# All query chunks weighed with v stationary, and their sums turned back into rows by 64-row transposes

## The chip, the cores and the metric

The kernel runs on one core of a Trainium2 chip. The metric is the device time of one execution in microseconds (us). The time before is 2366.17 us, the median of 3 runs (2365.53 to 2366.57).

## The reference

An attention without softmax, whose output goes through a mixture of experts that takes the best expert alone. Cut to what matters here:

```python
B, S, D, d_qk = 8, 2496, 256, 64
scores = (1 / S) * np.matmul(z, z.transpose(0, 2, 1))    # B x S x S
attn = np.maximum(scores, 0.0) ** 2
x = (u * np.matmul(attn, v)).reshape(B * S, D)
logits = x @ w_gate + modality_bias[modality_id]         # 8 experts
e_idx = np.argmax(logits, axis=1)
# out[i] = softmax(logits[i])[e_idx[i]] * (relu(x[i] @ w1[e]) @ w2[e]), e = e_idx[i]
```

All of it is float32. The kernel gets that precision from the faster float32r products by splitting both factors into a high and a low part and adding three products (high·high, high·low, low·high).

## The kernel before, in words

**Two phases.** Phase 1 computes the attention, the logits and the routing, and scatters the rows by expert to DRAM. Phase 2 takes tiles of 512 rows of one expert through the two layers. The change is in phase 1, but for one call in phase 2.

**Chunks and steps.** A batch entry has 2496 queries, in 5 chunks (c = 0 to 4) of 512, the last of 448. A chunk runs through its keys in 10 steps (i = 0 to 9) of two 128-key blocks, so phase 1 has 8 x 5 x 10 = 400 steps, numbered g. For a step:
- `scores` (L287) makes the products of keys and queries in 6 matmuls, 2 blocks x 3 terms, each on 64 rows of the array. The two blocks use the two halves of the array's rows (`halves`, partitions 0 to 63 and 64 to 127), so two matmuls run side by side, one in each half. ACT then applies the relu (L298) and the square (L304).
- `high` (L307) rounds the square to float32r on ACT or DVE (a table `by` chooses), and `low` (L314) takes the difference on DVE: `ah` and `al`, each 128 keys x 2 x 512 queries.
- `weigh` (L328) multiplies by v (`vh`, `vl`). The keys of the upper and lower 64 partitions are summed apart, in PSUM tiles `acc[r]` (r = 0, 1, the two halves of the array).

**Two forms of weigh.** For c < 4 (L341 to L358) the stationary operand is 128 queries of `ah` or `al` and the 256 columns of v move. The sums come out as rows (query on the partition). A step is 4 blocks of queries x 2 key blocks x 6 matmuls = 48 matmuls with 256 columns moving; the last step, whose second key block is only half real, has 36. For c = 4 (L359 to L369) the stationary operand is 128 columns of v and the 448 queries move: 24 matmuls, and the sums come out transposed (column of v on the partition).

**After a chunk.** `evacuate_low` (ACT, L391, two copies) and `evacuate_high` (DVE, L397, two additions) join the two halves' sums in the SBUF tile `x`. For c < 4, `gate_rows` (DVE, L403) then multiplies by u. For c = 4, `make_rows` (L407) turns the sums back into rows with eight 128x128 transposes on PE (L415), and `take_rows` (DVE, L422) multiplies them by u out of PSUM. Then come 16 pieces of `logits` (DVE, L432) and, once per batch entry, the routing.

**Order.** PE, ACT, DVE and POOL run in an order that the loop at L891 writes out. In iteration g it emits what is due, then `high(g+2)`, `scores(g+3)`, `low(g+2)`, `square(g+3)`, `weigh(g)` and the tasks fixed for g. The rest lies in queues with a first step and a last step, which `beside` empties as its estimates of ACT's and DVE's load allow. PSUM has one `s` tile of two banks and six banks for `acc`, of which a chunk takes four; the transposes take two of the same six.

Of the kernel before, what the change touches and what calls it, by code (L numbers as in the profile page):

```python
# [15 lines left out]
P = 128  # L16
T = 512
# [9 lines left out]
def tile_attention_moe(ctx: ExitStack, tc: tile.TileContext, u, v, zt, mid, wg, mb, w1, w2, out):  # L27
# [300 lines left out]
    def weigh(g):  # L328
# [6 lines left out]
        def terms(k):  # L335

            if k == NCOL - 1:
                return ((0, ah, 0), (1, ah, 0), (0, ah, 1))
            return tuple((r, x, y) for x, y in ((ah, 0), (ah, 1), (al, 0)) for r in range(2))

        if c < NCH - 1:  # L341

            for m in range(J):
                o = [acc[b, c][r][m // 2][:, m % 2 * D:(m % 2 + 1) * D] for r in range(2)]
                q = slice(m * P, (m + 1) * P)
                for t in range(2):
                    k = 2 * i + t
                    begins, ends = k == 0 and m % 2 == 0, k == NCOL - 1 and m % 2 == 1
                    for n, (r, x, y) in enumerate(terms(k)):
                        nc.tensor.matmul(  # L350
                            out=o[r],
                            lhsT=x[halves[r], t, q],
                            rhs=V[b, k // J][y][halves[r], k % J, :],
                            start=begins and n < 2,
                            stop=ends and y == 1 - r,
                            skip_group_check=True,
                        )
            return  # L358
        for dh in range(KD):  # L359
            for t in range(2):  # L360
                k = 2 * i + t
# [9 lines left out]

    oT, X, LG = {}, {}, {}

    EV = {}

    def evacuate_low(b, c, h):

        w = width[c]
        if not h:
            x = rows.tile([P, J, XW], F32, tag="x", bufs=NCH + 1, name="x")  # L380
            if c < NCH - 1:
                EV[b, c] = [x[:, 2 * n:2 * n + 2, 0:D] for n in range(J // 2)]
                X[b, c] = x
            else:
                t = x.rearrange("p j c -> p (j c)")[:, 0:KD * T].rearrange("p (k t) -> p k t", k=KD)
                nc.gpsimd.memset(t[:, :, w:T], 0.0)
                EV[b, c] = [t[:, n, :w] for n in range(KD)]
                oT[b, c] = (t, x)
        o = acc[b, c][1][h]
        o = o.rearrange("p (j d) -> p j d", d=D) if c < NCH - 1 else o[:, :w]  # L390
        nc.scalar.copy(out=EV[b, c][h], in_=o)  # L391

    def evacuate_high(b, c, h):
        o = acc[b, c][0][h]
        o = o.rearrange("p (j d) -> p j d", d=D) if c < NCH - 1 else o[:, :width[c]]
        y = EV[b, c][h]
        nc.vector.tensor_tensor(out=y, in0=o, in1=y, op=ALU.add)  # L397
        if h:
            acc.pop((b, c))

    def gate_rows(b, c):
        x, ut = X[b, c], U.pop((b, c))
        nc.vector.tensor_tensor(out=x[:, :, 0:D], in0=x[:, :, 0:D], in1=ut, op=ALU.mult)  # L403

    turned_rows = {}

    def make_rows(b, c):  # L407
        t, x = oT.pop((b, c))
        parts = []
        for h in range(J // 2):  # L410
            pt = bank_tile([P, 2, D], "po")
            for jj in range(2):
                for dh in range(KD):
                    j = 2 * h + jj
                    nc.tensor.transpose(out=pt[:, jj, dh * P:(dh + 1) * P], in_=t[:, dh, j * P:(j + 1) * P], identity=ident)  # L415
            parts.append(pt)
        turned_rows[b, c] = (parts, x)

    def take_rows(b, c):
        (parts, x), ut = turned_rows.pop((b, c)), U.pop((b, c))  # L420
        for h, pt in enumerate(parts):
            nc.vector.tensor_tensor(out=x[:, 2 * h:2 * h + 2, 0:D], in0=pt, in1=ut[:, 2 * h:2 * h + 2, :], op=ALU.mult)  # L422
        X[b, c] = x

    def logits(b, c, n):

# [241 lines left out]
    def at(g, f, *args):  # L668
        tasks.setdefault(g, []).append((f, args))
# [14 lines left out]
    for b in range(B):  # L684
# [9 lines left out]
        for c in range(NCH):  # L694
            g = g0 + c * NI
            at(g + 5, load_u, b, c)
            at(g + NI - 1, evacuate_low, b, c, 0)
            at(g + NI - 1, evacuate_low, b, c, 1)
            queue(g + NI, g + NI, dve(0.7, evacuate_high, b, c, 0))
            queue(g + NI, g + NI, dve(0.7, evacuate_high, b, c, 1))  # L700
            if c == NCH - 1 and b < B - 1:
                at(g + NI + 1, make_rows, b, c)
                queue(g + NI + 2, g + NI + 3, dve(1.4, take_rows, b, c))
            elif c < NCH - 1:
                queue(g + NI, g + NI + 1, dve(1.25, gate_rows, b, c))
            if b < B - 1 or c < NCH - 1:
                for n in range(LGN):
                    last = c == NCH - 1
                    queue(g + NI + (3 if last else 1), g + NI + (3 + n // 3 if last else 5 + n // 2), dve(0.35 * LG_STEP, logits, b, c, n))

    def routing(b):

# [322 lines left out]
            scatter(B - 1, k)  # L1035

    between[0][0] = [lambda: make_rows(B - 1, NCH - 1)]
    between[0][1] = [lambda: take_rows(B - 1, NCH - 1)]
# [60 lines left out]
```

## Time and profile before

| | us |
|---|---|
| median of the runs | 2366.17 |
| the profiled execution's own time | 2354.86 |
| its span, first to last instruction | 2353.1 |
| PE busy | 2312.9 (98%) |
| ACT busy | 1586.5 (67%) |
| DVE busy | 1558.6 (66%) |
| first weigh matmul of phase 1 / last | 17 / 1400 |

The profiled execution took 11.31 us less than the median of the runs. Busy time is the time in which an engine had an instruction in flight. Matmuls overlap in flight, so how fast PE goes is read from the starts of its instructions in the timeline, not from their durations.

### The profile page before, as it was taken

The page shows a single profiled execution, that of the slowest core. Times are in us where ns is not written, and L with a number is a line of the kernel's source. Part 1 is how long each engine was busy: PE and PEld are TensorE (multiplying, and loading weights), DVE is VectorE, ACT ScalarE, POOL GpSimd, SP SyncE. Part 2 cuts the span into 40 slices and gives each one's busy share as a digit, 9 for nine tenths or more (in the row PEclk, how much of TensorE's full clock was granted, in tenths as well). Part 3 has the DMA queues.
Part 4 walks back from the last instruction along what each step waited for, and adds up shares of the span by engine and source line. Part 5 has one row for each costly group of instructions (what it writes and reads, how often), then busy time and mean ns, then how long its engine had stood idle before and what let it go on. Part 6 is the DMA issues. An engine that isn't in the chain of part 4 may idle for free.

```text
span 2353.1 us, 58980 instructions
## 1 busy us (share of the span) xinstructions
PE 2312.9 (98%) x24092; PEld 2115.4 (90%) x24092; DVE 1558.6 (66%) x4305; ACT 1586.5 (67%) x1961; POOL 355.5 (15%) x350
## 2 busy tenths in 40 slices
PE   8999999999999999999999998999999999999996
PEld 7999999999999999999999996888888888888885
DVE  6888889889889889889889776333333333333432
ACT  7999999999999999999998862333333333333332
POOL 0000210210110210210210304111111111111111
PEclk9999999999999999999999999999999999999998
DMA  5332242232332331331321123511111431111110
GB/s 180 100 107 78 84 129 68 92 115 74 105 106 70 116 109 58 114 109 60 125 82 40 57 109 137 194 54 37 55 39 53 182 123 45 46 54 37 55 33 24
DMA packets 76185, 203.13 MB, mean 86 GB/s; under 512 B 16320, under 2 KB 26048, under 8 KB 73984
## 3 DMA queue, kind: packets, MB, share of 16 engines
q1 hardware_dynamic: 60768, 157.93, 20.5%
q0 software_dynamic: 15136, 41.34, 4.7%
q8 instruction: 190, 3.11, 0.6%
q14 instruction: 91, 0.75, 0.1%
HBM read 245.96 MB, written 79.10 MB: 138 GB/s over the span
## 4 chain that ended last, share of the span: by engine, by line
PE 95%; issue 1%; ACT 1%; DMA 1%; DVE 1%; POOL 0%; SPq 0%; POOLq 0%; ACTq 0%; DVEq 0%
PE acc L350 38%; PE ph L948 18%; PE s L296 12%; PE po L961 12%; PE acc L363 7%; PE po L962 6%; PE pt L806 1%; ACT r L298 0%; PE po L415 0%; DMA xs<-x,sloti 0%; DMA out_dram<-y,ids 0%; POOL xs L530 0%; ACT ah L311 0%; DMA vr<-in_v_dram 0%; POOL out_dram L980 0%
## 5 line engine op out<-in xcount | busy, mean ns | idle before, releaser
L350 PE MATMUL acc<-vh,ah 64*128 64x256 f32 x5120 | 867.6, 281 | 0.0
L350 PE MATMUL acc<-vl,ah 64*128 64x256 f32 x4992 | 860.0, 279 | 0.0
L350 PE MATMUL acc<-vh,al 64*128 64x256 f32 x4864 | 849.7, 279 | 0.0
L350 PEld LDWEIGHTS acc<-vh,ah 64*128 64x128 f32 x5120 | 685.7, 186 | 11.2 <-DVE x L397 0.2
L350 PEld LDWEIGHTS acc<-vl,ah 64*128 64x128 f32 x4992 | 661.1, 186 | 11.5
L350 PEld LDWEIGHTS acc<-vh,al 64*128 64x128 f32 x4864 | 654.5, 187 | 0.0
L952 ACT ACTIVATE hh<-ph 128x512 fp32r<-128x512 f32 (+1 forms) x320 | 189.6, 593 | 540.5 <-PE ph L948 540.5
L953 DVE SCALAR_TENSOR_TENSOR hl<-ph,hh 128x512 fp32r<-128x512 f32 (+1 forms) x320 | 218.9, 685 | 478.4 <-ACT hh L952 478.2
L320 DVE TENSOR_TENSOR al<-r,ah 128x1024 fp32r<-128x1024 f32 (+1 forms) x360 | 431.2, 1198 | 127.7 <-ACT ah L311 122.2
L432 DVE SCALAR_TENSOR_TENSOR spare<-x,wgb 128x256 f32<-128x256 f32 x1280 | 461.3, 420 | 0.6
L948 PE MATMUL ph<-xh,w 128*128 128x512 f32 (+1 forms) x1280 | 448.5, 397 | 10.0 <-DVE hl L953 9.4
L961 PE MATMUL po<-w,hh 128*128 128x512 f32 x1264 | 454.2, 394 | 0.0
L311 ACT CAST ah<-r 128x1024 fp32r<-128x1024 f32 (+1 forms) x371 | 381.4, 1028 | 77.6 <-PE acc L350 72.6
L304 ACT ACTIVATE r<-r 128x1024 f32<-128x1024 f32 (+1 forms) x400 | 415.9, 1040 | 12.7
L296 PE MATMUL s<-zm 64*128 64x512 f32 (+1 forms) x2400 | 405.8, 392 | 11.5 <-DVE zm L256 6.0
L298 ACT ACTIVATE r<-s 128x1024 f32<-128x1024 f32 (+1 forms) x400 | 400.2, 1000 | 17.4 <-PE s L296 13.2
L530 POOL DMA_INDIRECT xs<-x,sloti x160 | 194.2, 1214 | 1072.1 <-DVE x L528 968.0
L962 PE MATMUL po<-w,hl 128*128 128x256 f32 x1264 | 354.3, 281 | 0.0
L948 PEld LDWEIGHTS ph<-xh,w 128*128 128x128 f32 x1280 | 240.6, 189 | 65.5 <-DVE hl L953 10.7
L961 PEld LDWEIGHTS po<-w,hh 128*128 128x128 f32 x1264 | 237.6, 188 | 56.3 <-issue 0.2
L296 PEld LDWEIGHTS s<-zm 64*128 64x128 f32 x2400 | 260.4, 186 | 27.9 <-ACT r L298 10.2
L980 POOL DMA_INDIRECT out_dram<-y,ids x158 | 154.1, 975 | 728.9 <-DVE y L978 695.2
(143 smaller groups left out, 2439.1 us busy)
## 6 DMA issues: line engine op xcount, KB each, us to landing
w<-w1s SPq DMA_DIRECT2D x37, 2048.0 KB
w<-w2s SPq DMA_DIRECT2D x37, 2048.0 KB
xg<-xs SPq DMA_DIRECT2D x39, 516.0 KB
vr<-in_v_dram SPq DMA_DIRECT2D x32, 512.0 KB
ut<-in_u_dram SPq DMA_DIRECT2D x32, 512.0 KB
wraw<-in_moe_w_dram SPq DMA_DIRECT2D x64, 256.0 KB
w1s<-wpair SPq DMA_DIRECT2D x32, 512.0 KB
w2s<-wpair SPq DMA_DIRECT2D x32, 512.0 KB
```

Of the source, the lines that this page charges most:

```text
L296: nc.tensor.matmul(out=s[:, t, :w], lhsT=lhs, rhs=mv[halves[t], ql, :w], start=n == 0, stop=n == 2)
L298: nc.scalar.activation(out=r[:, :, :w], in_=s[:, :, :w], func=AF.Relu, scale=INV)
L304: nc.scalar.square(out=a[:, :, :w], in_=a[:, :, :w])
L311: copy(out=ah[:, :, :w], in_=st_a[g][:, :, :w])
L320: nc.vector.tensor_tensor(out=al[:, :, :w], in0=a[:, :, :w], in1=ah[:, :, :w].bitcast(F32), op=ALU.subtract)
L350: nc.tensor.matmul(out=o[r], lhsT=x[halves[r], t, q], rhs=V[b, k // J][y][halves[r], k % J, :], start=begins and n < 2, stop=ends and y == ...
L432: nc.vector.scalar_tensor_tensor(out=spare[:, k % 2, :], in0=x[:, j, 0:D], scalar=1.0, in1=wgb[:, e, :], op0=ALU.mult, op1=ALU.mult, accum ...
L530: nc.gpsimd.indirect_dma_start(out=xs, out_offset=bass.IndirectOffsetOnAxis(ap=RT[b]["sloti"][:n, k:k + 1], axis=0), in_=x[:n, j, :], in_o ...
L948: nc.tensor.matmul(out=ph, lhsT=lhs, rhs=rhs[:, k, :], start=n == 0, stop=n == 3 * KD - 1)
L953: nc.vector.scalar_tensor_tensor(out=hl, in0=ph, scalar=0.0, in1=hh.bitcast(F32), op0=ALU.max, op1=ALU.subtract)
L961: nc.tensor.matmul(out=po[j], lhsT=hh[:, s], rhs=both, start=f == 0, stop=False, skip_group_check=True)
L962: nc.tensor.matmul(out=po[j][:, 0:D], lhsT=hl[:, s], rhs=w[:, 0, :], start=False, stop=f == KF - 1, skip_group_check=True)
```

## The change

The form of weigh with the 256 columns of v moving is removed, and all chunks take the form of c = 4, with 512 queries moving (448 for c = 4). `gate_rows` is removed. `make_rows` now serves every chunk. In place of eight 128x128 transposes it makes sixteen of 64 rows, alternating between the halves of the array, each half into a PSUM bank of its own (`parts[r]`); `take_rows` has two calls, one for each bank. `make_rows` stands one step earlier than it did for c = 4, after the first weigh of the next chunk. The logits of c < 4 may begin one step later than before, those of c = 4 one step earlier.

```diff
-        if c < NCH - 1:
-
-            for m in range(J):
-                o = [acc[b, c][r][m // 2][:, m % 2 * D:(m % 2 + 1) * D] for r in range(2)]
-                q = slice(m * P, (m + 1) * P)
-                for t in range(2):
-                    k = 2 * i + t
-                    begins, ends = k == 0 and m % 2 == 0, k == NCOL - 1 and m % 2 == 1
-                    for n, (r, x, y) in enumerate(terms(k)):
-                        nc.tensor.matmul(
-                            out=o[r],
-                            lhsT=x[halves[r], t, q],
-                            rhs=V[b, k // J][y][halves[r], k % J, :],
...
-            return
...
             x = rows.tile([P, J, XW], F32, tag="x", bufs=NCH + 1, name="x")
...
+            t = x.rearrange("p j c -> p (j c)")[:, 0:KD * T].rearrange("p (k t) -> p k t", k=KD)
+            if w < T:
                 nc.gpsimd.memset(t[:, :, w:T], 0.0)
...
+            oT[b, c] = (t, x)
+        nc.scalar.copy(out=oT[b, c][0][:, h, :w], in_=acc[b, c][1][h][:, :w])
...
+        y = oT[b, c][0][:, h, :width[c]]
+        nc.vector.tensor_tensor(out=y, in0=acc[b, c][0][h][:, :width[c]], in1=y, op=ALU.add)
...
-    def gate_rows(b, c):
-        x, ut = X[b, c], U.pop((b, c))
-        nc.vector.tensor_tensor(out=x[:, :, 0:D], in0=x[:, :, 0:D], in1=ut, op=ALU.mult)
...
     def make_rows(b, c):
         t, x = oT.pop((b, c))
-        parts = []
-        for h in range(J // 2):
-            pt = bank_tile([P, 2, D], "po")
-            for jj in range(2):
-                for dh in range(KD):
-                    j = 2 * h + jj
-                    nc.tensor.transpose(out=pt[:, jj, dh * P:(dh + 1) * P], in_=t[:, dh, j * P:(j + 1) * P], identity=ident)
-            parts.append(pt)
+        parts = [bank_tile([P, J, KD, DK], "po") for _ in halves]
+        for j in range(J):
+            for dh in range(KD):
+                for r, h in enumerate(halves):
+                    nc.tensor.transpose(out=parts[r][:, j, dh, :], in_=t[h, dh, j * P:(j + 1) * P], identity=ident[h, h])
         turned_rows[b, c] = (parts, x)
...
+    def take_rows(b, c, r):
+
+        (parts, x), ut = turned_rows[b, c], U[b, c]
+
+        def of(a):
+            return a[:, :, 0:D].rearrange("p j (k h d) -> p j k h d", k=KD, h=2)[:, :, :, r, :]
+
+        nc.vector.tensor_tensor(out=of(x), in0=parts[r], in1=of(ut), op=ALU.mult)
...
-            if c == NCH - 1 and b < B - 1:
-                at(g + NI + 1, make_rows, b, c)
-                queue(g + NI + 2, g + NI + 3, dve(1.4, take_rows, b, c))
-            elif c < NCH - 1:
-                queue(g + NI, g + NI + 1, dve(1.25, gate_rows, b, c))
             if b < B - 1 or c < NCH - 1:
+                at(g + NI, make_rows, b, c)
+                for r in range(2):
+                    queue(g + NI + 1, g + NI + 2, dve(0.7, take_rows, b, c, r))
                 for n in range(LGN):
                     last = c == NCH - 1
-                    queue(g + NI + (3 if last else 1), g + NI + (3 + n // 3 if last else 5 + n // 2), dve(0.35 * LG_STEP, logits, b, c, n))
+                    queue(g + NI + 2, g + NI + (3 + n // 3 if last else 6 + n // 2), dve(0.35 * LG_STEP, logits, b, c, n))
```

How this moves the instructions is seen at two places. The first is PE's order in the first step of chunk 1 of batch entry 0, where the rows of chunk 0 are to be made. A row gives the line, the operation, the tile written and the tiles read (the moving one first), the size of what is written, and how many follow each other. Before:

```order
L350 MATMUL acc<-vh,ah 128x256 x2
L350 MATMUL acc<-vl,ah 128x256 x2
L350 MATMUL acc<-vh,al 128x256 x2
L296 MATMUL s<-zm 128x512 x6
L350 MATMUL acc<-vh,ah 128x256 x2
L350 MATMUL acc<-vl,ah 128x256 x2
L350 MATMUL acc<-vh,al 128x256 x2
```

The same place on PE in the changed kernel, where weigh is now at L345 and the transposes at L381:

```order
L345 MATMUL acc<-ah,vh 128x512 x2
L345 MATMUL acc<-ah,vl 128x512 x2
L345 MATMUL acc<-al,vh 128x512 x2
L381 MATMUL po<-ident,x 128x64 x16
L296 MATMUL s<-zm 128x512 x6
L345 MATMUL acc<-ah,vh 128x512 x2
L345 MATMUL acc<-ah,vl 128x512 x2
L345 MATMUL acc<-al,vh 128x512 x2
```

The sixteen transposes now stand between the weigh of the new chunk's first step and the next scores, and a row of weigh writes twice as many columns as before; a step has half as many such rows.

The second place is DVE's order after the same chunk, from its two evacuations on. Before:

```order
L397 TENSOR_TENSOR x<-acc,x 128x2x256 x2
L320 TENSOR_TENSOR al<-r,ah 128x1024
L403 TENSOR_TENSOR x<-x,ut 128x4x256
L320 TENSOR_TENSOR al<-r,ah 128x1024
L432 SCALAR_TENSOR_TENSOR spare,lg<-x,wgb 128x256 x8
L320 TENSOR_TENSOR al<-r,ah 128x1024
```

In the changed kernel, where the evacuation is at L369, `take_rows` at L391 and the logits at L403, DVE has there:

```order
L369 TENSOR_TENSOR x<-acc,x 128x512 x2
L320 TENSOR_TENSOR al<-r,ah 128x1024 x2
L391 TENSOR_TENSOR x<-po,ut 128x4x2x64 x2
L320 TENSOR_TENSOR al<-r,ah 128x1024
L403 SCALAR_TENSOR_TENSOR spare,lg<-x,wgb 128x256 x8
L320 TENSOR_TENSOR al<-r,ah 128x1024
```

The one multiplication by u has become two that read PSUM, and one more `low` (L320) stands ahead of them.

More of the change, by code (lines that the diff above doesn't have):

```diff
@@ L372, in tile_attention_moe @@
     oT, X, LG = {}, {}, {}
-    EV = {}
     def evacuate_low(b, c, h):
@@ L408, in make_rows @@
         t, x = oT.pop((b, c))
[L409 to L423 removed]
+        parts = [bank_tile([P, J, KD, DK], "po") for _ in halves]
[3 more added lines that the diff above has]
+                    nc.tensor.transpose(out=parts[r][:, j, dh, :], in_=t[h, dh, j * P:(j + 1) * P], identity=ident[h, h])
+        turned_rows[b, c] = (parts, x)
+    def take_rows(b, c, r):
[3 more added lines that the diff above has]
+        nc.vector.tensor_tensor(out=of(x), in0=parts[r], in1=of(ut), op=ALU.mult)
+        if r:
+            del turned_rows[b, c], U[b, c]
+            X[b, c] = x
     def logits(b, c, n):
@@ L1037, in tile_attention_moe @@
     between[0][0] = [lambda: make_rows(B - 1, NCH - 1)]
-    between[0][1] = [lambda: take_rows(B - 1, NCH - 1)]
+    between[0][1] = [lambda: take_rows(B - 1, NCH - 1, 0), lambda: take_rows(B - 1, NCH - 1, 1)]
     for n in range(LGN):
```

18 lines of the change are left out of this document (removed).

## The prediction

> **What bounds the kernel now.** The page comes first: the span, the busy engines, the chain that ended last.
>
> ```profile
> span 2353.1 us, 58980 instructions
> PE 2312.9 (98%) x24092; PEld 2115.4 (90%) x24092; DVE 1558.6 (66%) x4305; ACT 1586.5 (67%) x1961; POOL 355.5 (15%) x350
> ...
> PE 95%; issue 1%; ACT 1%; DMA 1%; DVE 1%; POOL 0%; SPq 0%; POOLq 0%; ACTq 0%; DVEq 0%
> PE acc L350 38%; PE ph L948 18%; PE s L296 12%; PE po L961 12%; PE acc L363 7%; PE po L962 6%; PE pt L806 1%; ACT r L298 0%; PE po L415 0%; DMA xs<-x,sloti 0%; DMA out_dram<-y,ids 0%; POOL xs L530 0%; ACT ah L311 0%; DMA vr<-in_v_dram 0%; POOL out_dram L980 0%
> ```
>
> PE is 95% of the chain, and the largest line in it is the weigh that the change replaces (L350, 38%). An average over two phases hides how near the others are, so next comes the busy time of phase 1 alone (the columns are the stretch, its length, and each engine's busy time).
>
> ```profile
> 10.00:1400.00 1390.00, 1386.85 (x19319) 1334.88 (x19320) 1183.49 (x3541) 1280.19 (x1401) 179.80 (x158) 1.00 0.29 95
> ```
>
> In phase 1 ACT is busy 92% and DVE 85%. PE waits almost never, so what PE issues per step is the time, but ACT has little room.
>
> **What a step costs on PE.** The pace is in the starts of the timeline's rows (start, length, line, what, shape, count; x2 is a pair, one matmul in each half of the array). One step of chunk 0 to 3, and the scores of the steps beside it:
>
> ```profile
> 892.65 0.86 PE L296 MATMUL s<-zm 64*128 64x512 f32 x6
> 893.35 0.28 PE L350 MATMUL acc<-vh,ah 64*128 64x256 f32 x2
> 893.47 0.28 PE L350 MATMUL acc<-vl,ah 64*128 64x256 f32 x2
> ...
> 896.10 0.28 PE L350 MATMUL acc<-vh,al 64*128 64x256 f32 x2
> 896.22 0.86 PE L296 MATMUL s<-zm 64*128 64x512 f32 x6
> 896.92 0.28 PE L350 MATMUL acc<-vh,ah 64*128 64x256 f32 x2
> ...
> 903.37 0.86 PE L296 MATMUL s<-zm 64*128 64x512 f32 x6
> ```
>
> Three steps from 892.65 to 903.37 are 3.573 us each. The 24 pairs of weigh start 893.35 to 896.10, 23 gaps in 2.75: 0.1196 a pair of 256 columns. The three pairs of scores, 512 columns, take 896.22 to 896.92: 0.233 each. Chunk 4 already has the form that all chunks get, with 448 columns:
>
> ```profile
> 853.97 0.36 PE L363 MATMUL acc<-ah,vh 64*128 64x448 f32 x1
> 854.17 0.36 PE L363 MATMUL acc<-ah,vl 64*128 64x448 f32 x1
> ...
> 857.00 0.36 PE L363 MATMUL acc<-ah,vh 64*128 64x448 f32 x1
> ```
>
> From one step's first matmul to the next one's are 3.03 us for 12 pairs of weigh and 3 of scores: 0.202 a pair. So a pair costs a little more than its columns: 0.467 ns a column at 256, 0.451 at 448. That surplus is what the change saves.
>
> **Full steps of chunks 0 to 3** (32 chunks x 9 = 288). In proportion to 448, a pair of 512 columns takes 0.202 x 512/448 = 0.231. Ends: 0.2295 (64 columns more at the slope between 256 and 448, 0.43 ns) and 0.233 (the scores above). A step is then 15 x 0.231 = 3.465 (3.44 to 3.495) for 3.573: 0.108 less, x288 = **-31.1 us** (-38 to -22).
>
> The Trainium skill, "TensorE: Matmul & The Clock Gate", section "Back-to-back issue gap", speaks against this: an isolated matmul's gap is its columns at 2.4 GHz and a fixed 2.5 ns. By that halving the number of pairs saves 12 x 2.5 = 30 ns a step, 8.6 us in all. The rows disagree: 256 columns at that rate are 107 ns, and the pair took 119.6. The result by that rule stands below as a rival.
>
> **Last steps** (32). One half of the array issues 20 matmuls before and 10 after: 20 x 0.1196 - 10 x 0.231 = 0.08, **-2.6 us**.
>
> **The new transposes.** Chunk 4 shows the old ones, eight of 128x128 among 64-row work, on PE and in the weight loads (PEld):
>
> ```profile
> 887.75 0.28 PE L350 MATMUL acc<-vh,al 64*128 64x256 f32 x2
> 887.96 1.10 PE L415 MATMUL po<-ident,x 128*128 128x128 f32 x8
> 888.98 0.96 PE L296 MATMUL s<-zm 64*128 64x512 f32 x6
> 889.78 0.28 PE L350 MATMUL acc<-vh,ah 64*128 64x256 f32 x2
> ```
>
> ```profile
> 887.95 0.14 PEld L415 LDWEIGHTS po<-ident,x 128*128 128x128 f32 x1
> ```
>
> ```profile
> 887.95 0.20 PEld L415 LDWEIGHTS po<-ident,x 128*128 128x128 f32 x2
> ```
>
> Seven gaps lie in 1.10 less the last one's own 0.27 (1.10 / 8 would count the flight): 0.11 to 0.12 a transpose. The two PEld rows are windows that end after the first and after the second load: 0.20 - 0.14 says that on the empty array the second load began 0.06 after the first. So the array takes such a load each 0.06, and the 0.11 is the 128 moving columns of the identity. The new ones move 64. No row shows a pair of 64-row transposes. Below: eight pairs at 0.06, 0.5 us a chunk. Above, if pairs go side by side as in weigh: 0.12, the pace at which PE took four instructions per pair there, 0.95 a chunk. If the halves don't overlap: sixteen at 0.06 to 0.11, 1.0 to 1.8. I take 0.09 a pair, between the first two, since two 64-row loads go side by side in every pair of weigh: 0.7 a chunk, x32 = **+22.4 us** (16 to 30, 58 if serial).
>
> The Trainium skill, "TensorE: Matmul & The Clock Gate", section "LDWEIGHTS (loading the stationary operand)", prices a load at its columns over 1.2, 107 ns for these 128; by that eight pairs are 0.85 a chunk and this term 27 us. The gap of 0.06 above speaks against it for this kind of load.
>
> **Chunk 4's own transposes** (7 in phase 1). The last pair before them would end its slot at 887.87; scores start at 888.98, 1.11 later, and take 0.80 up to the weigh instead of 0.70: 1.21 in all, since the array changes from 64 to 128 rows and back. After, everything around is 64 rows, so the same 0.7: 7 x (0.7 - 1.21) = **-3.6 us**. The eighth, in phase 2, now stands as 64-row work among 128-row matmuls: two changes of rows, about 0.1 each by this row, **+0.2**.
>
> **What lies beside PE.** A chunk's boundary on ACT and DVE (952.91 is the start of the old chunk's last pair):
>
> ```profile
> 952.91 0.28 PE L350 MATMUL acc<-vl,ah 64*128 64x256 f32 x1
> ...
> 956.36 0.39 PE L296 MATMUL s<-zm 64*128 64x512 f32 x1
> ```
>
> ```profile
> 953.05 1.06 ACT L391 COPY x<-acc 128x512 f32<-128x512 f32 x2
> ...
> 954.94 1.04 ACT L298 ACTIVATE r<-s 128x1024 f32<-128x1024 f32 x1
> ```
>
> ```profile
> 953.65 1.29 DVE L397 TENSOR_TENSOR x<-acc,x 128x512 f32<-128x512 f32 x2 [1.26 <-ACT x L391]
> ```
>
> The transposes wait for DVE's second evacuation, done at 954.94. PE will come to them after one more step, 952.91 + 0.12 + 3.47 = 956.5: 1.6 us to spare. The latest evacuation is that after chunk 0, where routing stands ahead of it on DVE:
>
> ```profile
> 918.58 1.29 DVE L397 TENSOR_TENSOR x<-acc,x 128x512 f32<-128x512 f32 x2
> ```
>
> ```profile
> 920.74 0.97 PE L296 MATMUL s<-zm 64*128 64x512 f32 x6
> ```
>
> Done at 919.87, with PE at its next scores at 920.74: 0.8 to spare. Behind the transposes PE's queue holds the next scores, and so ACT's relu; that is what a wait would delay.
>
> With one `s` tile, scores wait for the last relu. At the boundary it ends at 955.98, 0.38 before the scores of 956.36: the tightest place. There PE now spends 0.7 more, so the margin grows; elsewhere steps lose 0.11 of it. Of the 400 casts (L311) the new order gives ACT 386, before 371: 15 x 1.05 = 16 us more in 1390, 94% busy. I cost both at nothing; without that cover each 0.1 us of wait per chunk is 4 us.
>
> DVE: `gate_rows` goes, two readings of PSUM come:
>
> ```profile
> L403 DVE TENSOR_TENSOR x<-x,ut 128x1024 f32<-128x1024 f32 x32 | 39.0, 1220 | 0.0
> L422 DVE TENSOR_TENSOR x<-po,ut 128x512 f32<-128x512 f32 x16 | 10.3, 682 | 0.0
> ```
>
> 2 x 0.682 - 1.220 = 0.14 x 32 = 4.6 us on an engine with 207 us free in phase 1. They stand behind one more `low`, by when the transposes are over. Scatters and loads of u follow `take_rows`, a step later; nothing in the chain hangs on them. Cost nothing.
>
> **Sum.** -31.1 - 2.6 + 22.4 - 3.6 + 0.2 = -14.7 us on the profiled execution's 2354.86, so 2340.2. Its own time is 11.31 below the median of the runs, 2366.17, and the same distance gives 2351.5. With t us of transposes a chunk the sum is -42 + 39 t, and breaks even at t = 1.08. About 0.2%, 4.7 us, is what a measurement of this kernel tells from no change.
>
> **The rivals.**
> - *More than that*: pairs at 0.06 and at 0.2295 in weigh, and waits at boundaries covered. -42 - 7 + 20 = -29: 2337. For it speaks the load gap of 0.06; against it, that no row shows PE take four instructions in 0.06. Chance 0.12.
> - *Transposes at the instruction pace*, t = 0.95, or serial at 0.06, t = 1.0: -5 to -3, so 2361 to 2363. For it speaks the 0.12 of weigh's pairs. Chance 0.18.
> - *Slower, because the two halves take turns* in transposes, each at the 0.11 of a 128-row one: t = 1.8, +28: 2394. It decides from t = 1.08. Against it speak the pairs that share every start in the rows above. Chance 0.08.
> - *The weigh isn't faster*: the columns alone set the pace, and a pair of 512 takes two of 256, 0.239. The sum keeps +22.4 - 3.6 + 0.2 = +19: 2385. The scores' 0.233 and the 0.202 of 448 speak against it. Chance 0.05. By the fixed 2.5 ns of the Trainium skill ("TensorE: Matmul & The Clock Gate", "Back-to-back issue gap") it would be +19 - 8.6 = +10.4, 2377.
> - *A new wait* at each boundary, PE standing at the transposes for DVE or at the scores for ACT: 0.5 us x 39 = +19.5 turns the sum to +5: 2371. Against it speak the margins of 0.8 to 1.6. Chance 0.07.
>
> **How the numbers follow.** The forecast, t between 0.6 and 0.9, has 0.5: 2347 to 2359, likeliest 2351.5. With the two rivals that are also not slower it makes 0.80, so the range is 2337 to 2364. Faster by over 0.2%: 0.5 + 0.12 + half of 0.18 = 0.71; within: the other 0.09 and a part of the new wait, 0.13; slower: 0.16.
>
> **What would show it.** Steps of chunks 0 to 3 that are 3.44 to 3.50 apart by their scores prove the first term; 3.57 refutes it. The distance from weigh's last pair to the scores at a boundary gives t. If L381 or the scores after it have idle time before them with DVE or ACT as releaser, the new wait is real. Phase 2's length should stay within 1 us. The forecast is wrong if t is above 1.08 or the pair of 512 above 0.236.

## The result and the profile after

The changed kernel takes 2351.35 us (median of 6 runs, 2349.41 to 2352.19) beside 2366.14 for the kernel before (6 runs, 2364.90 to 2366.57): a ratio of 0.9937, 95% interval 0.9924 to 0.9950, so 14.8 us or 0.6% faster. The forecast was 2351.5. The sum was right to a fraction of a microsecond; its terms were not, and this part is mostly about them. The profiled execution took 2351.21, its span is 2349.4.

The page of the changed kernel, first the span and the busy times, then the chain that ended last:

```profile
span 2349.4 us, 45178 instructions
PE 2288.8 (97%) x17180; PEld 2035.9 (87%) x17180; DVE 1550.2 (66%) x4322; ACT 1595.4 (68%) x1976; POOL 373.5 (16%) x350
...
PE 85%; DVE 8%; ACT 3%; issue 2%; another core or an unknown queue 1%; DMA 0%; POOL 0%; SPq 0%; DVEq 0%; POOLq 0%; ACTq 0%
```

PE issues 6912 matmuls less and is still the bound, but DVE has come into the chain, 8% for 1% before: PE now waits for it somewhere. The busy time of phase 1 (stretch, length, then PE, PEld, DVE, ACT, POOL):

```profile
10.00:1390.00 1380.00, 1366.37 (x12426) 1258.62 (x12427) 1176.48 (x3561) 1290.88 (x1418) 198.37 (x158) 1.00 0.29 95
```

PE stands 13.6 us in this stretch; in the one of before it stood 3.2.

**Weigh.** A full step of the changed kernel on PE's timeline, chunk 2:

```profile
951.96 0.96 PE L296 MATMUL s<-zm 64*128 64x512 f32 x6
952.65 0.50 PE L345 MATMUL acc<-ah,vh 64*128 64x512 f32 x2
...
955.17 0.50 PE L345 MATMUL acc<-al,vh 64*128 64x512 f32 x2
955.39 0.97 PE L296 MATMUL s<-zm 64*128 64x512 f32 x6
...
962.26 0.96 PE L296 MATMUL s<-zm 64*128 64x512 f32 x6
```

From 951.96 to 962.26 are three steps: 3.433 us each, for 3.573 before. Twelve pairs of weigh start from 952.65 to 955.17, 0.229 apart, and the three of scores take 0.69, 0.23 each. So 0.140 x 288 = 40.3 us are gone from the full steps.

**Transposes.** The same boundary of chunks, a step earlier:

```profile
947.66 0.28 PE L381 MATMUL po<-ident,x 64*128 64x64 f32 x2
947.88 0.75 PE L381 MATMUL po<-ident,x 64*128 64x64 f32 x12
948.44 0.47 PE L296 MATMUL s<-zm 64*128 64x512 f32 x1
948.47 0.28 PE L381 MATMUL po<-ident,x 64*128 64x64 f32 x2
948.56 0.93 PE L296 MATMUL s<-zm 64*128 64x512 f32 x5
```

The sixteen start between 947.66 and about 948.53, and the first of the next scores starts among them, at 948.44, in the half of the array that is done. They have no idle time before them. What they cost has to come from an experiment, since the halves overlap.

**A wait that was not forecast.** At the boundary of chunk 0 and 1, PE and then DVE (the number in brackets is the idle time and what ended it):

```profile
910.22 0.39 PE L345 MATMUL acc<-ah,vh 64*128 64x512 f32 x1
911.66 0.50 PE L345 MATMUL acc<-ah,vh 64*128 64x512 f32 x1 [1.06 <-DVE x L369]
...
912.94 0.69 PE L381 MATMUL po<-ident,x 64*128 64x64 f32 x13
```

```profile
907.66 1.22 DVE L320 TENSOR_TENSOR al<-r,ah 128x1024 fp32r<-128x1024 f32 x1
908.79 0.32 DVE L445 SCALAR_TENSOR_TENSOR val<-sh,em 128x160 f32<-128x160 f32 x1
...
910.64 0.17 DVE L461 CAST cnt<-run 128x8 fp32r<-128x8 f32 x1
910.92 1.29 DVE L369 TENSOR_TENSOR x<-acc,x 128x512 f32<-128x512 f32 x2
```

DVE is busy back to back: `low` (L320), then routing (L445 to L461), then the evacuation (L369), whose first half ends at 911.56. PE has stood since 910.61 for it, not at the transposes but 1.3 us ahead of them, in the middle of the new chunk's first step: its second six pairs of weigh need PSUM banks of the old chunk (six starts lie between the stop and the transposes). PE's waits in the whole execution (total, times, longest), of the changed kernel and of the kernel before:

```profile
PE ph L917 <- DVE hl L922: 16.6, 1, 16.6
PE s L296 <- ACT r L298: 7.7, 9, 2.6
PE acc L345 <- DVE x L369: 7.0, 7, 1.1
```

```profile
PE ph L948 <- DVE hl L953: 9.4, 1, 9.4
...
PE s L296 <- ACT r L298: 5.2, 4, 2.6
```

The third row is new, 7.0 us, once for each batch entry but the first, in which there is no routing yet; the wait for relu has grown from 5.2 to 7.7. The first row belongs to phase 2.

**Phase 1 and phase 2 apart.** The last matmul of weigh, before and after:

```profile
1400.18 0.36 PE L363 MATMUL acc<-ah,vl 64*128 64x448 f32 x1
```

```profile
1386.19 0.36 PE L345 MATMUL acc<-ah,vl 64*128 64x448 f32 x1
```

Phase 1 ends 13.99 us earlier. From there to the end of the span are 2353.1 - 1400.18 = 952.9 us before and 963.2 after, 10.3 more, though the code there changed by sixteen transposes. Most of that is the first row of the waits: PE stood 9.4 us once early in phase 2 in the execution of before, and 16.6 after. The first experiment asks whether the change did that.

### The profile page after: what moved, and what is told of

Same layout as the page of the kernel before. It is cut to its first block, busy times and chain, and to the rows that moved or that the text cites. A ratio compares the mean times of both kernels' runs of the same rounds, so it can differ in the third digit from the quotient of the medians.

```text
span 2349.4 us, 45178 instructions
## 1 busy us (share of the span) xinstructions
PE 2288.8 (97%) x17180; PEld 2035.9 (87%) x17180; DVE 1550.2 (66%) x4322; ACT 1595.4 (68%) x1976; POOL 373.5 (16%) x350
## 4 chain that ended last, share of the span: by engine, by line
PE 85%; DVE 8%; ACT 3%; issue 2%; another core or an unknown queue 1%; DMA 0%; POOL 0%; SPq 0%; DVEq 0%; POOLq 0%; ACTq 0%
PE acc L345 37%; PE ph L917 18%; PE po L930 12%; PE s L296 10%; PE po L931 6%; DVE spare L403 3%; DVE al L320 2%; PE pt L775 1%; DVE vl L271 1%; PE po L381 1%; ACT r L298 1%; ACT ah L311 1%; ACT r L304 0%; ACT vh L265 0%
## 5 line engine op out<-in xcount | busy, mean ns | idle before, releaser
L345 PE MATMUL acc<-ah,vh 64*128 64x512 f32 (+1 forms) x3200 | 771.0, 382 | 7.0 <-DVE x L369 7.0
L345 PE MATMUL acc<-ah,vl 64*128 64x512 f32 (+1 forms) x3120 | 760.3, 384 | 0.3 <-DVE vl L271 0.3
L345 PE MATMUL acc<-al,vh 64*128 64x512 f32 (+1 forms) x3040 | 737.7, 384 | 0.0
L922 DVE SCALAR_TENSOR_TENSOR hl<-ph,hh 128x512 fp32r<-128x512 f32 (+1 forms) x320 | 219.0, 685 | 498.9 <-ACT hh L921 494.2
L320 DVE TENSOR_TENSOR al<-r,ah 128x1024 fp32r<-128x1024 f32 (+1 forms) x360 | 431.1, 1197 | 154.0 <-ACT ah L311 147.0
L345 PEld LDWEIGHTS acc<-ah,vh 64*128 64x128 f32 x3200 | 448.4, 185 | 36.3 <-DVE x L369 10.0
L917 PE MATMUL ph<-xh,w 128*128 128x512 f32 (+1 forms) x1280 | 448.5, 397 | 18.7 <-DVE hl L922 16.6
L403 DVE SCALAR_TENSOR_TENSOR spare<-x,wgb 128x256 f32<-128x256 f32 x1280 | 462.6, 421 | 0.9
L345 PEld LDWEIGHTS acc<-ah,vl 64*128 64x128 f32 x3120 | 436.6, 184 | 26.5 <-DVE vl L271 0.7
L345 PEld LDWEIGHTS acc<-al,vh 64*128 64x128 f32 x3040 | 424.0, 184 | 21.9
L311 ACT CAST ah<-r 128x1024 fp32r<-128x1024 f32 (+1 forms) x386 | 396.8, 1028 | 59.9 <-PE acc L345 56.9
L296 PE MATMUL s<-zm 64*128 64x512 f32 (+1 forms) x2400 | 387.9, 391 | 14.6 <-ACT r L298 7.7
L501 POOL DMA_INDIRECT xs<-x,sloti x160 | 212.8, 1330 | 1037.7 <-DVE x L499 901.9
L296 PEld LDWEIGHTS s<-zm 64*128 64x128 f32 x2400 | 276.0, 186 | 38.4 <-ACT r L298 15.0
L917 PEld LDWEIGHTS ph<-xh,w 128*128 128x128 f32 x1280 | 240.4, 188 | 75.6 <-DVE hl L922 19.2
```

The lines of the kernel that those rows point to most:

```text
L296: nc.tensor.matmul(out=s[:, t, :w], lhsT=lhs, rhs=mv[halves[t], ql, :w], start=n == 0, stop=n == 2)
L311: copy(out=ah[:, :, :w], in_=st_a[g][:, :, :w])
L320: nc.vector.tensor_tensor(out=al[:, :, :w], in0=a[:, :, :w], in1=ah[:, :, :w].bitcast(F32), op=ALU.subtract)
L345: nc.tensor.matmul(out=acc[b, c][r][dh][:, :w], lhsT=V[b, k // J][y][halves[r], k % J, dh * P:(dh + 1) * P], rhs=x[halves[r], t, :w], star ...
L403: nc.vector.scalar_tensor_tensor(out=spare[:, k % 2, :], in0=x[:, j, 0:D], scalar=1.0, in1=wgb[:, e, :], op0=ALU.mult, op1=ALU.mult, accum ...
L501: nc.gpsimd.indirect_dma_start(out=xs, out_offset=bass.IndirectOffsetOnAxis(ap=RT[b]["sloti"][:n, k:k + 1], axis=0), in_=x[:n, j, :], in_o ...
```

## The experiments

Times are medians. Each is set beside runs of the kernel before on the same chip, and that kernel took 2366 us on some chips and 2354 on others; so ratios are compared, or ends of phase 1 (the start of the last matmul of weigh), which hardly depend on the chip: 1400.18 and, in the first experiment, 1399.76.

**The kernel before, unchanged.** No edit.

> The kernel before, unchanged, for a second profile. Its first profiled execution took 2354.86 us, the runs 2366. Theory A: that execution was lucky at one place, the start of the first tile of phase 2 (PE idle 9.4 us there), and a typical one shows about 20 us lost there: span near 2364, with phase 1 ending within 1 us of 1400 as before. Rival B: the 11 us lie spread over phase 1 or phase 2: phase 1 ends at 1405 or later, or all of phase 2's tiles are longer.

It took 2365.33 us beside 2366.01, ratio 0.9997 (0.9987 to 1.0008). PE's longest wait in its profile:

```profile
PE ph L948 <- DVE hl L953: 20.0, 1, 20.0
```

Its phase 2 has 2363.4 - 1399.76 = 963.6 us, 0.4 more than that of the changed kernel and 10.7 more than in the first profile. The stop of PE early in phase 2 is in the kernel before as well, of 9.4 us in one execution and 20.0 in another. The 11.31 us between the first profile and the median were this, and the change has no part in it.

**The evacuation earlier in DVE's queue.** The second number is the step from which a piece is taken ahead of the others:

```diff
-            queue(g + NI, g + NI, dve(0.7, evacuate_high, b, c, 0))
-            queue(g + NI, g + NI, dve(0.7, evacuate_high, b, c, 1))
+            queue(g + NI, g + NI - 9, dve(0.7, evacuate_high, b, c, 0))
+            queue(g + NI, g + NI - 9, dve(0.7, evacuate_high, b, c, 1))
```

> The changed kernel, with the two evacuations on DVE put ahead of everything else that is due in their step (at the boundary from chunk 0 to 1 the routing stood ahead of them). Theory: PE's wait for the evacuation there, 1.06 us in 7 batch entries, is new, made by the faster weigh meeting a full DVE, and goes: 2342 to 2346. Rival: DVE is full through that whole stretch, so what is moved behind (the routing, the low parts) makes PE wait instead: 2349 to 2353.

It took 2341.41 us, ratio 0.9898 (0.9882 to 0.9915), a little below the theory's 2342, and on another chip, later, 2339.66, ratio 0.9893 (0.9877 to 0.9910):

> The changed kernel with the earlier evacuation, unchanged from its first run, beside the kernel with the row behind the four, to compare the two on one chip. If this chip has the short stop of PE early in phase 2 (9.4 us, the kernel before at 2354), 2328 to 2332; if it has the long one (17 to 20 us, the kernel before at 2366), 2340 to 2343.

DVE's rows at the same boundary, and PE's there:

```profile
901.85 1.22 DVE L320 TENSOR_TENSOR al<-r,ah 128x1024 fp32r<-128x1024 f32 x1
902.99 1.29 DVE L369 TENSOR_TENSOR x<-acc,x 128x512 f32<-128x512 f32 x2
904.19 0.32 DVE L445 SCALAR_TENSOR_TENSOR val<-sh,em 128x160 f32<-128x160 f32 x1
```

```profile
905.36 0.28 PE L381 MATMUL po<-ident,x 64*128 64x64 f32 x2
905.58 0.76 PE L381 MATMUL po<-ident,x 64*128 64x64 f32 x12
```

The evacuation now stands ahead of routing (L445), and PE no longer waits for it. Phase 1 ends at 1375.67, 10.5 us earlier than in the changed kernel, more than the 7.0 of the wait. The profile counts a wait from the end of the last matmul in flight, so a stop is longer than its wait. By the first scores of neighbouring steps, the first step of chunk 1, in which PE stood, takes 4.22 us in the mean in place of 5.48: 10.1 us over the eight batch entries. That the order on DVE was the cause is shown; the queue alone changed.

**No transposes.** Leaves out those of chunks 0 to 3; `take_rows` multiplies u by itself there.

```diff
+        if c < NCH - 1:
+            turned_rows[b, c] = (None, x)
+            return
...
-        nc.vector.tensor_tensor(out=of(x), in0=parts[r], in1=of(ut), op=ALU.mult)
+        nc.vector.tensor_tensor(out=of(x), in0=parts[r] if parts else of(ut), in1=of(ut), op=ALU.mult)
```

> The changed kernel without the transposes of chunks 0 to 3 (left out: the attention's sums there; u is multiplied by itself in their place, so the work of every other engine stays). It prices the transposes themselves. Theory: 32 x 0.45 us = 14 us, less what DVE takes back at the boundary of chunk 0: 2337 to 2342. Rival, the forecast's 0.7 a chunk: 22 us: 2329.

It took 2336.59 us, ratio 0.9876 (0.9860 to 0.9893). Phase 1 ends at 1371.22, 14.97 us before 1386.19, so the transposes of 32 chunks cost 0.47 us each, 0.058 a pair. The boundary wait stayed (7.1 us), so this is the price of the transposes beside it. It is the net price: in this run the last three steps of chunk 4 take 3.8 us more than in the changed kernel (summed over the batch entries, from the first scores of neighbouring steps), so in their own place the transposes cost more, about 18.8 us or 0.59 a chunk.

**The old transposes for all chunks.** The weigh of the change, with eight 128x128 transposes a chunk instead of sixteen of 64 rows:

```diff
-                for r, h in enumerate(halves):
-                    nc.tensor.transpose(out=parts[r][:, j, dh, :], in_=t[h, dh, j * P:(j + 1) * P], identity=ident[h, h])
+                    nc.tensor.transpose(out=pt[:, jj, dh * P:(dh + 1) * P], in_=t[:, dh, j * P:(j + 1) * P], identity=ident)
```

> The changed kernel, but all chunks turned by eight 128x128 transposes as chunk 4 was before. Theory: a chunk's turn costs 1.2 us instead of some 0.5, since the array changes from 64 to 128 rows and back and each transpose moves 128 columns: 39 x 0.7 = 27 us, of which PE's wait at a few boundaries hides a part: 2368 to 2379. Rival: 64-row transposes run no faster than the forecast's 0.7 to 0.95, so 10 to 20 us: 2361 to 2368.

It took 2372.80 us, ratio 1.0031 (1.0019 to 1.0042): slower than the kernel before, as the theory said. Its phase 1 ends at 1407.27, 21.1 us later than that of the changed kernel. So of the two forms of transposes the faster weigh pays only with the one in halves.

**One half of the array at a time.** The same sixteen transposes in another order:

```diff
-        for j in range(J):
-            for dh in range(KD):
-                for r, h in enumerate(halves):
+        for r, h in enumerate(halves):
+            for j in range(J):
+                for dh in range(KD):
```

> The changed kernel with its sixteen transposes of a chunk in another order: the eight of the first half of the array, then the eight of the second. Same instructions, same number. Theory: t is only 0.46 us a chunk because a transpose in one half runs beside the next one in the other half; eight in a row in one half then follow each other at 0.06 to 0.11, so t is 1.0 to 1.8 and the kernel is 17 to 43 us slower than the changed one: 2368 to 2394. Rival: the sixteen go at the pace of issue wherever they stand (0.03 each): 2351 within 3.

It took 2344.90 us beside 2354.45, ratio 0.9958 (0.9942 to 0.9973). A boundary on PE:

```profile
951.19 0.77 PE L381 MATMUL po<-ident,x 64*128 64x64 f32 x13
951.74 0.50 PE L296 MATMUL s<-zm 64*128 64x512 f32 x1
951.80 0.35 PE L381 MATMUL po<-ident,x 64*128 64x64 f32 x3
```

Phase 1 ends at 1390.84, 4.65 us later than in the changed kernel: 0.12 for each of its 39 chunks, not the 0.5 to 1.3 of the theory. Thirteen start within 0.77 - 0.22 = 0.55 us, 0.046 apart in the mean. Windows of the timeline that end 0.01 us later each time give the single starts: one each 0.06 us from 951.19 to 951.37, then two at 951.43, one at 951.49, and two each at 951.55 and 951.61. Two that start together must lie in different halves of the array, so the second half's transposes run beside the first's from the fifth start on. The theory had the pace of one half right (0.06) and the sum wrong: it let the second half wait for the first. In the changed kernel the same windows show two starts at 948.28 and two at 948.34. So in both orders t is low because one of these transposes is short and because the two halves overlap; alternating them adds little. The rival, no difference, is nearer but not right either.

**Chunk 4 alone in halves.** The kernel before, with the sixteen transposes for chunk 4 only (the `make_rows` of the change, and the two multiplications of `take_rows` in one piece).

> The kernel before with one part of the change: chunk 4's rows are turned by 64-row transposes in the two halves; chunks 0 to 3 keep the weigh in rows. The prediction's term was -3.6 + 0.2 us; with the 0.46 us a chunk that the runs showed for the new transposes it is 7 x (0.46 - 1.21) = -5.3 us. So 2360 to 2363, with the last weigh of phase 1 some 4 to 6 us earlier than 1400. Rival: the change of rows in the array costs nothing, and the gain is only the 64 columns less: 8 x 0.06 x 7 = 3.4 us at most, 2362.5 to 2366.

It took 2352.98 us beside 2354.45, ratio 0.9994 (0.9985 to 1.0003), which is no difference that can be told. Phase 1 ends at 1398.27, 1.9 us earlier than in the first profile of the kernel before and 1.5 earlier than in the second, where 4 to 6 were expected. At the place itself the transposes cost what they should:

```profile
886.64 0.66 PE L413 MATMUL po<-ident,x 64*128 64x64 f32 x16
887.10 0.96 PE L296 MATMUL s<-zm 64*128 64x512 f32 x6
```

They occupy 0.46 us up to the scores, where the eight of before took 1.02. But the waits have a new row:

```profile
PE acc L350 <- DVE x L397: 1.7, 6, 0.6
```

PE came earlier to the next boundary and met DVE's evacuation there. By the first scores of neighbouring steps, the step with the transposes takes 0.58 us less than in the kernel before, 4.6 us over the eight batch entries, and the first step of chunk 1, where the wait is, takes 0.40 more, 3.2 us. So the gain was made at its place, and two thirds of it were lost one boundary later. The ratio lies where the rival had it, but the rival's reason, that the change of rows costs nothing, does not fit the 4.6.

**The planner's step.** It estimates with 3.56 us what a full step takes; PE now needs 3.43. On top of the earlier evacuation:

```diff
-            after = now + 3.56 * scale
+            after = now + 3.44 * scale
```

> The changed kernel with the earlier evacuation (2341.4), and the planner's step of 3.56 us set to 3.44, the one that PE now has. It then gives ACT 8 casts fewer. Theory: PE's remaining waits for ACT's relu (some 0.45 us at the steps around chunk 4, 7.7 us in all) come from a planner that believes ACT has 0.12 us a step more than it has; they fall below 4 us and the kernel takes 2336 to 2341. Rival: the casts only move the wait to DVE, whose evacuations come later again: 2341 to 2347.

It took 2363.41 us beside 2354.45, ratio 1.0039 (1.0023 to 1.0054): 1.4% slower than the same kernel with 3.56 (0.9898), with phase 1's end at 1403.73 for 1375.67. Neither expectation held. PE's waits:

```profile
PE s L296 <- ACT r L298: 11.3, 22, 2.4
PE s L296 <- DVE zm L256: 10.8, 7, 6.1
PE acc L345 <- DVE vl L271: 10.6, 13, 1.3
```

PE now waits for the pieces that prepare z and v (L256, L271), 21.4 us in all, where with 3.56 it waited 6.4. The reading is that with the true step the planner sees less room, leaves these pieces until they are due, and PE arrives first; where they stand in its order was not compared. The step of 3.56 then works not as an estimate of PE but as a margin. The other way, 3.70, on top of the spread scatters below:

> The kernel with the spread scatters (2316.3 beside 2354.5 for the kernel before), and the planner's step at 3.70 instead of 3.56, the other way from the trial with 3.44. Theory: with 3.44 the pieces that prepare z and v stood until they were due, and PE waited for them; with 3.70 they stand earlier, and PE's waits in phase 1 get fewer: ratio to the kernel before 0.980 to 0.984. Rival: the planner then gives ACT more casts than it has time for, relu comes late, and the ratio is 0.985 to 0.992.

It took 2371.86 us, ratio 1.0031 (1.0020 to 1.0042), worse again, and by another wait:

```profile
PE pc L467 <- DVE x L391: 22.5, 7, 3.2
```

The matmul that counts tokens for routing (L467) stands in PE's queue right behind the transposes. One of the seven places on PE and on DVE, and the windows around it (the third number from the end is PE's granted clock):

```profile
400.63 0.72 PE L381 MATMUL po<-ident,x 64*128 64x64 f32 x16
404.52 0.37 PE L467 MATMUL pc<-cnt,below 128*128 128x8 f32 x1 [3.17 <-DVE x L391]
...
406.49 0.63 PE L345 MATMUL acc<-ah,vh 64*128 64x512 f32 x2
```

```profile
397.18 0.17 DVE L461 CAST cnt<-run 128x8 fp32r<-128x8 f32 x1
...
403.78 1.28 DVE L391 TENSOR_TENSOR x<-po,ut 128x512 f32<-128x512 f32 x2
```

```profile
400.00:401.00 1.00, 1.00 (x19) 0.98 (x17) 0.81 (x1) 0.97 (x2) 0.00 (x0) 1.00 0.00 0
401.00:406.00 5.00, 1.83 (x17) 1.54 (x15) 3.21 (x7) 1.58 (x2) 0.00 (x0) 0.83 0.00 0
406.00:411.00 5.00, 5.00 (x26) 3.85 (x24) 0.72 (x3) 2.08 (x2) 0.00 (x0) 0.50 0.34 105
```

The counts were ready 7 us earlier, at 397.35. What released the matmul is `take_rows` (L391): the matmul's tile `pc` is one of the same six banks of PSUM, and the transposes' tiles hold theirs until `take_rows` has read them. In this order `take_rows` stands behind a `low` that itself waits for a cast on ACT.

Here the stop of 3.17 us goes with nearly 7 us at half the clock (0.50, from 404.3 to 411), in which a pair takes 0.42 and not 0.23, so it costs its 3.2 and some 3 more. The seven stops are alike in length (3.17 to 3.24), but not in what follows: windows of 1 us show the clock at 0.50 for 6.8 us at two of them and for 3.4 at the other five. That makes about 2 x (3.2 + 3.4) + 5 x (3.2 + 1.7) = 38 us, and phase 1 ended at 1414.72 for 1374.59, 40.1 later. The other 15.6 us by which this run is longer lie in phase 2 (below).

**The stop in phase 2.** It is there before and after the change, so it has no part in the result, but it is the largest wait left. In the first profile of the kernel before it reads, on POOL and on DVE:

```profile
1453.74 0.92 POOL L530 DMA_INDIRECT xs<-x,sloti  x1 [0.30 <-issue]
1454.96 0.98 POOL L980 DMA_INDIRECT out_dram<-y,ids  x1 [0.30 <-issue]
```

```profile
1457.47 0.48 DVE L978 SCALAR_TENSOR_TENSOR y<-po,xg,part 128x256 f32<-128x256 f32 x1 [8.65 <-DMA out_dram<-y,ids]
```

The results of phase 2's first tile wait on POOL behind the last batch entry's 20 scatters of 1.28 us. There are six `y` buffers, the first tile holds four, and the third `y` of the second tile stands until one has left. That is the stop of 9.4 us. The long stop goes another way; in the profile that has 20.0 us, on ACT and DVE:

```profile
1462.89 1.08 ACT L952 ACTIVATE hh<-ph 128x512 fp32r<-128x512 f32 x2 [23.38 <-remote]
```

```profile
1463.52 0.69 DVE L953 SCALAR_TENSOR_TENSOR hl<-ph,hh 128x512 fp32r<-128x512 f32 x1 [22.24 <-ACT hh L952]
1472.44 0.48 DVE L978 SCALAR_TENSOR_TENSOR y<-po,xg,part 128x256 f32<-128x256 f32 x1 [0.22 <-ACT part L976]
```

Here the third `y` waits for no buffer. PE stands for DVE's `hl`, `hl` for ACT's `hh`, and ACT, while the scatters run, for something that the trace does not name ("remote" is another core or an unknown queue). All six profiles with a stop of 14.6 to 20.0 us have such waits on ACT, 21.9 to 28.3 us, and none for a `y` buffer; in the four with 9.4 to 9.7 it is the other way round. What ACT waits for stays open.

Two kernels changed the order of the scatters. The first spreads them over the two next tiles, behind each of their steps, and moves the loading of a tile behind them:

```diff
-        for k in range(NCOL):
-            scatter(B - 1, k)
...
+        for k in range(NCOL):
+            between[1 + k // (KF + 2)].setdefault(k % (KF + 2), []).append(lambda k=k: scatter(B - 1, k))
...
```

> The changed kernel with the earlier evacuation (2341.4), and the last batch's 20 scatters, which stand in one row on POOL at the end of phase 2's first tile, spread over its next two tiles, one behind each step; loading of tile 0 follows them. Theory: PE's stop of some 17 us early in phase 2 is there because its instructions come late behind the row of scatters; with two steps' time between scatters the stop shrinks below 6 us, and the kernel takes 2326 to 2334. Rival: the stop belongs to the place in PE's program, and stays: 2339 to 2344.

It took 2316.34 us beside 2354.45, ratio 0.9838 (0.9823 to 0.9853). The row `PE ph L917 <- DVE hl L922` is gone from its waits, and its phase 2 has 2313.3 - 1374.59 = 938.7 us, where the kernel before has 952.9 with the short stop. Yet POOL took the first fifteen scatters in one row, 1.28 apart; what had changed for these is that the first tile's four results stood ahead. The second kernel therefore changes the order alone:

```diff
-        for k in range(NCOL):
-            scatter(B - 1, k)
...
+    def last_scatters():
+        for k in range(NCOL):
+            scatter(B - 1, k)
...
+        between[1][0] = [last_scatters]
```

> The changed kernel with the earlier evacuation, and the last batch's 20 scatters one place later: behind the four scatters of phase 2's first tile on POOL, not ahead of them, but still in one row. Theory: PE's stop comes from the order on POOL. The first tile's four results wait behind the row of 20 x 1.28 us, their buffers come free late, and what needs a free buffer holds DVE and then PE. So the stop goes without any spreading: as fast as the kernel with the spread scatters, 14 us (11 to 17) below the earlier evacuation alone on a chip with the short stop, 20 to 27 on one with the long stop. Rival: the stop comes from the density of the scatters, and stays: within 4 us of the earlier evacuation alone.

This came to a chip with the long stop: 2331.11 us beside 2365.39, ratio 0.9857 (0.9840 to 0.9873), 8.6 below the earlier evacuation alone (2339.66). That is less than the 20 to 27 of the theory and more than the 4 of the rival. Its phase 2 has 954.4 us, and that of the earlier evacuation alone 960.7 on this chip. The wait for `hl` is gone here too, but PE still stands, and by nothing that the trace names:

```profile
1430.08 0.79 PE L930 MATMUL po<-w,hh 128*128 128x512 f32 x1 [7.56 <-issue]
```

So the order on POOL has a part in the long stop too, 6.3 us of it here; by what way is not shown, since the third `y` waited for no buffer. Whether spreading removes the rest was to be told by the first kernel on a chip with the long stop:

> The kernel with the spread scatters, unchanged. With the row behind the four in one piece, on a chip with the long stop, phase 2 took 954.4 us from the last weigh to the end, and PE still stood some 13 us there, most of it with nothing that it waited for; with the spread scatters it took 938.7, on a chip with the short stop. Theory: spreading takes away the rest of the stop as well, on either chip: phase 2 of 938 to 943, a ratio of 0.979 to 0.984 to the kernel before if that takes 2366, 0.982 to 0.986 if 2354. Rival: on a chip with the long stop PE stands as with the row in one piece: phase 2 of 948 to 956, ratio 0.985 to 0.988. If the chip has the short stop, this stays open.

It met a chip with the short one: 2315.43 us beside 2354.64, ratio 0.9834 (0.9817 to 0.9850). The gain is repeated. The question is answered by the run with the planner's step at 3.70: it has the spread scatters too, with the same program in phase 2, and ran on the chip with the long stop. Its phase 2 took 2369.0 - 1414.72 = 954.3 us, as much as with the scatters in one row behind the four (954.4), and ACT waited 13.2 and 7.2 us for "remote" in it. So spreading takes away the short stop and not the rest of the long one, as the rival said. Among the kernels tried, this one, with the earlier evacuation and the spread scatters, is the fastest.

## Why the prediction was right

By its own steps, with ends of phase 1 where an experiment gives them:

| step | forecast, us | measured, us | from |
|---|---|---|---|
| full steps of chunks 0 to 3 | -31.1 (-38 to -22) | -40.3 | 288 x (3.433 - 3.573) |
| last steps | -2.6 | not measured apart | |
| new transposes | +22.4 (16 to 30) | +15.0; in their place +18.8 | without them |
| chunk 4's transposes | -3.6 | -4.6 | chunk 4 alone, at the place |
| boundary, PE for DVE | 0 | +10.5 | earlier evacuation |
| scores for ACT's relu | 0 | +2.5 | 7.7 - 5.2 in the waits |
| phase 2 | +0.2 | -0.4 | the kernel before again |

With the -2.6 as forecast and +15.0 for the transposes, phase 1's terms add to -19.5; it ended 14.0 earlier. Two places account for these 5.5 us and 0.8 more, which is open. The transposes cost 3.8 more in their place. And the -40.3 counts 0.140 for all 288 steps, which holds in the middle of a chunk; by the first scores of neighbouring steps, the 24 second steps of chunks 1 to 3 gained 0.8 us together and not 3.4.

*Weigh* had the right mechanism and too small a size: the -40.3 is beyond its own end of -38, and with 2.5 less for the second steps it lies at that end. The pair of 512 takes 0.229, under the 0.2295 to 0.233 that were given as ends, and all fifteen pairs of a step have it. The step of 3.433 came out just below the 3.44 to 3.50 that were to prove the term. The estimate in proportion to 448 columns scaled the fixed part of a pair along with its columns. From 256 columns at 0.1196 and 448 at 0.202, each further column costs 0.43 ns; from there to 512 it is 0.42. The rule of the fixed 2.5 ns, in the Trainium skill ("TensorE: Matmul & The Clock Gate", "Back-to-back issue gap"), is for an isolated matmul; the estimate by it was 8.6 us. The steps gave 40.3, so these pairs do not follow it.

*The new transposes* cost 0.47 us a chunk, or 0.59 in their place, not 0.7; in all 15.0 us, just under the range of 16 to 30, or 18.8, inside it. The lower bound, the 0.06 between two loads on the empty array, was the right row; I moved away from it for the pace at which weigh issues four matmuls, and that is no limit here. The case with the halves in turn, 58 us, was priced wrongly as well: the order of one half after the other costs 4.65.

*What lies beside PE* is the step that failed: it put the boundary at nothing, and it cost 10.5 us. It measured the margins at the transposes (1.6 and 0.8 us) and at the scores (0.38). PE stands earlier than at either, in the first step of the new chunk, for a bank of `acc`. That chunk 0's evacuation stands behind routing was seen, and its end was read from the old timeline; but PE now comes to the boundary earlier, and DVE, which is full there, does not. Of the rivals, the cheap weigh and transposes of *more than that* (-29) and *a new wait* came true together; the wait at seven boundaries and not at 39. Without it the kernel would have been at the 2341 of the earlier evacuation, close to that rival's 2337.

*Chunk 4's transposes* were right at their place (4.6 for 3.6), and in the kernel before most of that was lost again at the next boundary.

*The distance of 11.31 us* to the median was kept as it was, without a reason, and that came out right: it is the longer stop in phase 2, which both kernels have. Phase 2 kept within 1 us, as was said, against a profile of the kernel before with that stop.

So the number was hit by luck: the errors to one side (7 to 9 us too little gain from weigh, 4 to 7 too much cost of the transposes, 1 too little from chunk 4) nearly cancel the 13 us of waits that had no price. The sign was safer: at 0.47 to 0.59 us a chunk the transposes are far from the 1.08 at which the sum broke even.

## What to carry to other kernels

When the engine that bounds a kernel gets faster, look for each thing that it takes from an engine that is full at that place, PSUM banks too, and compare the moments of need with the other engine's old times; a margin of less than the time gained until there is gone. Work that frees a bank belongs ahead of work that nobody waits for yet, and one number in a queue was worth as much here as two thirds of the change. And profile the kernel before twice before carrying a distance between profile and median: here it was a stop that depends on the chip.

## What the runs showed of the hardware

- A 64-row fp32 transpose of 64 columns follows the last in its half of the array after 0.06 us, though each is on record with 0.21 to 0.28 us. The 128-row one of 128 columns takes 0.11 to 0.12.
- A pair of 64-row matmuls, one in each half of the array, follows the last after 0.1196, 0.202 and 0.229 us at 256, 448 and 512 moving columns.
- At seven stops of 3.17 to 3.24 us PE's granted clock fell to 0.50, five times for 3.4 us and twice for 6.8; at the 1.06 us of the boundary it stayed at 1.00. The Trainium skill ("TensorE: Matmul & The Clock Gate", "What's actually happening") gives half the clock after an idle window of about 3.4 us. The trace agrees as far as it goes: from the start of the last transpose to the start of L467 the stops are 3.39 to 3.46 us.
- PE's stop in phase 2 is 9.4 us for the kernel before in one execution and 20.0 in another, with the same program; in the kernels that have the same order on POOL it was 9.4 to 9.7 where the kernel before takes 2354 us and 14.6 to 20.0 where it takes 2366. In the long one ACT waits 21.9 to 28.3 us for something that the trace does not name. That this comes from the traffic of the scatters was suspected and not shown.
